# A linear-attention stage: projections in plain fp32 on quarters of the array

## The chip, the cores and the metric

The kernel runs on one core of one Trainium2 chip. The metric is the device time of one execution in microseconds, median over runs; smaller is better. The engines are named as in the profile: PE is TensorE (PEld its weight loads), DVE VectorE, ACT ScalarE, POOL GpSimd, SP the queue that issues most DMAs.

## The reference, cut to what matters

Three layers follow each other: an attention with random features, a soft mixture of experts, and a second mixture. The change touches the first only.

```python
# q, k, v: (4, 8, 576, 64); w_phi: (64, 128)
def phi(x):
    proj = np.einsum('bhsd,df->bhsf', x, w_phi)
    proj = proj - np.max(np.abs(proj), axis=-1, keepdims=True)
    return np.concatenate([np.exp(proj), np.exp(-proj)], axis=-1)
q_p, k_p = phi(q), phi(k)
kv = np.einsum('bhsf,bhsd->bhfd', k_p, v)
z = np.sum(k_p, axis=2)
num = np.einsum('bhsf,bhfd->bhsd', q_p, kv)
den = np.einsum('bhsf,bhf->bhs', q_p, z)[..., None] + 1e-06
return num / den
```

The result, 2304 tokens of 512, goes into `_moe_ref` (logits against `phi`, softmax over tokens and over slots, eight experts on 4 slots each) and then `_moe2_ref` (eight experts of 512 x 1024 on all tokens).

## The kernel before, in words

The 2304 tokens are 18 blocks of 128. A batch has 576 tokens, so blocks 4 and 13 straddle two batches. The attention stage is one loop (lines 444 to 505) in which iteration `i` works on block `i` of k and on block `t = i - 7` of q: iterations 0 to 6 have k alone, up to 17 both, from 18 on q alone.

A block of k or q comes transposed as 128 x 512 fp32 (`kt`, `qt`): 128 rows are the 64 features of two heads, and four pairs `p` of heads stand side by side. `wbd` is a block-diagonal 128 x 256 matrix with `w_phi` twice, so that one product projects both heads of a pair. `split` (lines 120 to 131) makes a high part in fp32r (ACT) and a low part (POOL, for the first two k blocks DVE); `project` (133 to 152) adds three products for each pair: high by high, high by the low part of `wbd`, low by high. A PSUM tile holds four heads, `hh` the first or second half of the eight. DVE takes the largest absolute value of each head off (lines 148 and 150), ACT makes the exponentials.

For k, `kv_acc` adds up v times the features in PSUM over the blocks of a batch, two heads side by side in the column halves of the array, and `z_acc` adds the features up in SBUF (on POOL; while `t < LAG` POOL and DVE take half each). At a batch's end `kv_finish` turns the sums: `kvp` multiplies them by `bd`, which holds an identity and the routing matrix `phi` of the next layer, `zc` brings the z sums into columns; both go into `kvs`, 97 columns for each head.

For q, `q_transpose` turns the projected block by products with an identity, and `q_num` multiplies its exponentials by `kvs` (line 271), for each batch in the block apart; then DVE divides, sums the logits and writes the attention's output `x`. `slot_inputs` turns groups of four blocks into the slots' inputs between these steps.

In this part a planner at compile time decides the order on each engine, from its own costs and the order of the program; after the loop (line 506) the order of the program holds. Loads are issued by SP in order: k, v, q, and 1 MB units of the mixtures' weights among them, into buffers that come free as the stage goes on (`wk` after the last k block, `wq` after the last q block). The next stage begins at line 510.

Of the kernel before, what the change touches and what calls it, by code (L numbers as in the profile page):

```python
# [7 lines left out]
F32 = mybir.dt.float32  # L8
F32R = mybir.dt.float32r
# [6 lines left out]
F = 128  # L16
# [37 lines left out]
def tile_kernel(ctx: ExitStack, tc: tile.TileContext, a):  # L54
# [46 lines left out]
    kt_t, qt_t, vt_t = {}, {}, {}  # L101

    def load_k(t):
        x = kp.tile([128, 512], F32, tag="kt", name=f"kt{t}")
        SP.dma_start(out=x, in_=a["kT"][t])
        kt_t[t] = x

# [3 lines left out]
        vt_t[i] = x  # L111

    def load_q(t):
        x = qp.tile([128, 512], F32, tag="qt", name=f"qt{t}", bufs=2)
        SP.dma_start(out=x, in_=a["qT"][t])
        qt_t[t] = x

    parts = {}

    def split(src, pool, nm, t):  # L120

        hi = pool.tile([128, 512], F32R, tag=f"{nm}h", name=f"{nm}h{t}", bufs=1)
        lo = pool.tile([128, 512], F32R, tag=f"{nm}l", name=f"{nm}l{t}", bufs=1)
        if nm == "k" and t == 0:
            V.tensor_copy(out=hi, in_=src)
        else:
            A.copy(out=hi, in_=src)
        yield
        (V if nm == "k" and t < 2 else G).tensor_tensor(out=lo, in0=src, in1=hi.bitcast(F32), op=ALU.subtract)
        parts[nm, t] = hi, lo  # L130
        yield

    def project(pool, nm, t):

        hi, lo = parts.pop((nm, t))
        pss, us = [], []
        for hh in range(2):
            ps = mm(f"p{nm}{t}_{hh}")
            for j in range(2):
                p = 2 * hh + j  # L140
                o, s = ps[:, j * 256:(j + 1) * 256], slice(p * 128, (p + 1) * 128)
# [3 lines left out]
            pss.append(ps)  # L145
        for hh in range(2):
            m = pool.tile([128, 4], F32, tag=f"m{nm}", name=f"m{nm}{t}_{hh}", bufs=4)
            V.tensor_reduce(out=m, in_=h4(pss[hh]), axis=AX.X, op=ALU.max, apply_absolute_value=True)
            u = pool.tile([128, 512], F32, tag=f"u{nm}", name=f"u{nm}{t}_{hh}", bufs=2)
            V.tensor_tensor(out=h4(u), in0=h4(pss[hh]), in1=m.unsqueeze(2).to_broadcast([128, 4, F]), op=ALU.subtract)  # L150
# [5 lines left out]
    kvacc = {}  # L156

    def k_project(t):
        uk_t[t] = project(kp, "k", t)

    def k_exp(t):
        us = uk_t.pop(t)
        phik = kp.tile([128, H, 2, F], F32, tag="phik", name=f"phik{t}")
        for hh in range(2):
# [36 lines left out]
    def kv_finish(b):  # L201

        acc = kvacc.pop(b)
        kvt = kp.tile([128, 1024], F32, tag="kvt", name=f"kvt{b}", bufs=1)
        for i in range(2):
            A.copy(out=kvt[:, i * 512:(i + 1) * 512], in_=acc[:, i * 512:(i + 1) * 512])
        yield
        zs = zs_t.pop(b)
        zp = mm(f"zp{b}")
        for g in range(4):  # L210
            PE.matmul(zp[32 * g:32 * g + 32, :], ones[:, 0:32], zs[:, g * 512:(g + 1) * 512], start=True, stop=True)
        zrow = kp.tile([128, 512], F32, tag="zrow", name=f"zrow{b}", bufs=1)
        V.tensor_copy(out=zrow, in_=zp)
        kvs = qp.tile([128, 2, H, XW], F32, tag=f"kvs{b % 2}", name=f"kvs{b}", bufs=1)
        for p in range(4):
            ps = mm(f"kvp{b}_{p}")
            for c in range(2):
                PE.matmul(ps[:, c * 192:(c + 1) * 192], kvt[:, p * 256 + c * 128:p * 256 + (c + 1) * 128], bd[:, p], start=True, stop=True)  # L218
            src = ps[:, 0:384].rearrange("p (c h w) -> p c h w", c=2, h=2)
            for c in range(2):  # L220
                dst = kvs[:, c, 2 * p:2 * p + 2, 0:XW - 1]
                if c == 0:
                    A.copy(out=dst, in_=src[:, c])
                else:
                    V.tensor_copy(out=dst, in_=src[:, c])
        zc = mm(f"zc{b}")
        for j in range(2):
            for c in range(2):
                o = (j * 2 + c) * 4
                PE.matmul(zc[:, o:o + 4], zrow[:, j * 256 + c * 128:j * 256 + (c + 1) * 128], sel_e, start=True, stop=True)  # L230

        for c in range(2):
            V.tensor_copy(
                out=kvs[:, c, :, XW - 1].rearrange("p (g j) -> p j g", j=2),
                in_=zc[:, 0:16].rearrange("p (j c g) -> p j c g", j=2, c=2)[:, :, c, :],
            )
        kvs_t[b] = kvs
        yield

    def q_project(t):  # L240
        uq_t[t] = project(qp, "q", t)

    def q_transpose(t, hh):
        ps = mm(f"ut{t}_{hh}")
# [15 lines left out]
    def q_num(t, hh):  # L260
        if hh == 0:
            x_t[t] = const.tile([128, DM], F32, tag=f"x{t % XR}", name=f"x{t}", bufs=1)
        phiq = phiq_t.pop((t, hh))
        if hh == 0:
            lgh_t[t] = qp.tile([128, H, NS], F32, tag="lgh", name=f"lgh{t}", bufs=1)
        lgh = lgh_t[t]
        ps = mm(f"num{t}_{hh}")
        for b, r0, r1 in parts_of(t):
            for j in range(4):
                for c in range(2):  # L270
                    PE.matmul(  # L271
                        ps[r0:r1, j * XW:(j + 1) * XW],
                        phiq[:, c, j * 128 + r0:j * 128 + r1],
                        kvs_t[b][:, c, 4 * hh + j, :],
                        start=c == 0, stop=c == 1,
                    )
# [12 lines left out]
        def x_part():  # L289
            (in_order(V) if held else V).tensor_tensor(  # L290
                out=x_t[t][:, hh * 256:(hh + 1) * 256].rearrange("p (h d) -> p h d", h=4),
                in0=pv[:, :, 0:D], in1=rd.to_broadcast([128, 4, D]), op=ALU.mult,
            )

        if held:
            held_x.append(x_part)
        else:
            x_part()
# [95 lines left out]
        V.tensor_tensor(out=cc, in0=cc, in1=rm.to_broadcast([128, n, NS]), op=ALU.mult)  # L394

    load_k(0)
    wbd = kp.tile([128, 512], F32, tag="zrow", name="wbd", bufs=1)[:, 0:2 * F]
    SP.dma_start(out=wbd, in_=a["wbd"])
    load_k(1)
    load_v(0)  # L400
# [14 lines left out]
    wbdh = qp.tile([128, 2 * F], F32R, name="wbdh", bufs=1)  # L415
    wbdl = qp.tile([128, 2 * F], F32R, name="wbdl", bufs=1)
    A.copy(out=wbdh, in_=wbd)
    V.tensor_tensor(out=wbdl, in0=wbd, in1=wbdh.bitcast(F32), op=ALU.subtract)
# [12 lines left out]
    def k_split(t):
        return split(kt_t.pop(t), kp, "k", t) if t < NT else iter(())

    def q_split(t):
        return split(qt_t.pop(t), qp, "q", t) if 0 <= t < NT else iter(())

    LAG = 7
    for _ in k_split(0):
        pass
    k_project(0)  # L440
    for _ in k_split(1):
        pass
    k_exp(0)
    for i in range(NT + LAG + 1):
        t = i - LAG
# [14 lines left out]
        if i + 1 < NT:  # L460
# [585 lines left out]
```

## Time and profile before

| | us |
|---|---|
| median of 3 runs | 1073.94 |
| lowest, highest | 1071.92, 1074.38 |
| span of the profiled execution | 1066.3 |
| PE busy in it | 1039.9 |
| DVE busy | 734.3 |
| POOL busy | 688.3 |
| ACT busy | 571.5 |

The span runs from the first to the last instruction that was recorded; the runs' times hold what lies around it as well. The profiled execution has no other time than its span; the median stands 7.6 us above it. Matmuls are pipelined and their ends are modelled, so PE's busy time is not work alone; distances from one start to the next are of more use.

### The profile page before, as it was taken

Reading aid. Unit: us, or ns where it says so; the run is one execution under the profiler, and the core shown is the slowest. Engines: PE = TensorE matmul, PEld = TensorE weight load, DVE = VectorE, ACT = ScalarE, POOL = GpSimd, SP = SyncE. Lnnn points to the kernel's source line nnn. Section 1 sums busy time; section 2 is a strip of 40 time slices with the busy share of each in tenths; the row PEclk is TensorE's granted clock in tenths of the full one; section 3 lists DMA queues with packets and bytes.
Section 4 is the critical chain, followed back from the end, with each engine's and each line's share of the span. In section 5 each row is a group of like instructions: output and inputs, shape, how many; then the busy total and the mean of one; then the engine's idle time right before and its main releaser. Section 6 shows DMA issues by size and latency. Waiting matters only on the chain.

```text
span 1066.3 us, 23151 instructions
## 1 busy us (share of the span) xinstructions
PE 1039.9 (98%) x9206; PEld 974.1 (91%) x9206; DVE 734.3 (69%) x1518; ACT 571.5 (54%) x1009; POOL 688.3 (65%) x442
## 2 busy tenths in 40 slices
PE   7999999999899999999999999999999999999998
PEld 5688878963799999999999999999999999999998
DVE  6878787850578867667666767676667667676765
ACT  5665544412556666665556555554655565555542
POOL 4776561106656776777778578767867785787543
PEclk9999999999999999999999999999999999999999
DMA  8773215469400040022003100400210031000111
GB/s 261 252 278 88 60 35 184 166 263 409 190 2 1 2 159 1 2 82 78 2 1 120 41 2 2 159 2 1 90 70 1 2 120 41 2 1 21 56 45 61
DMA packets 22571, 89.26 MB, mean 84 GB/s; under 512 B 2752, under 2 KB 5568, under 8 KB 14272
## 3 DMA queue, kind: packets, MB, share of 16 engines
q1 hardware_dynamic: 22176, 87.26, 22.8%
q8 instruction: 73, 1.20, 0.5%
q0 software_dynamic: 288, 0.52, 0.2%
q14 instruction: 34, 0.28, 0.1%
HBM read 83.05 MB, written 4.72 MB: 82 GB/s over the span
## 4 chain that ended last, share of the span: by engine, by line
PE 90%; DVE 4%; POOL 2%; issue 2%; DMA 2%; ACT 1%; SPq 0%; DVEq 0%; POOLq 0%; ACTq 0%
PE x L50 36%; PE y L50 18%; PE z L50 15%; PE num L271 6%; PE kvacc L179 2%; PE ut L246 1%; PE ps L50 1%; PE kvp L218 1%; DMA moe_w<-in_moe_w 1%; PE ph L50 1%; PE pk L142 1%; PE pk L144 1%; POOL zs L197 1%; PE pq L142 1%; PE pq L144 1%
## 5 line engine op out<-in xcount | busy, mean ns | idle before, releaser
L50 POOL TENSOR_TENSOR hl_s<-s,hh_s 128x512 fp32r<-128x512 f32 x288 | 367.5, 1298 | 215.9 <-ACT hh_s L50 195.8
L50 ACT ACTIVATE hh_s<-s 128x512 fp32r<-128x512 f32 x288 | 176.3, 630 | 55.5 <-DVE s L50 51.6
L50 PE MATMUL x<-w_t,hh_s 128*128 128x256 f32 x1152 | 204.2, 277 | 0.0
L50 ACT ACTIVATE r<-z 128x512 f32<-128x512 f32 x144 | 86.2, 599 | 165.6 <-PE z L50 165.3
L50 PEld LDWEIGHTS x<-w_t,hh_s 128*128 128x128 f32 x1152 | 173.5, 188 | 0.1
L50 DVE SCALAR_TENSOR_TENSOR xo<-x,P,xo 128x256 f32<-128x256 f32 x252 | 120.8, 479 | 70.6 <-PE x L50 70.6
L50 ACT ACTIVATE hh_a<-z 128x512 fp32r<-128x512 f32 x216 | 122.3, 600 | 74.9 <-DVE s L50 74.1
L50 PE MATMUL x<-w_t,hl_s 128*128 128x256 f32 x576 | 159.2, 276 | 0.0
L50 DVE SCALAR_TENSOR_TENSOR s<-z,r 128x512 f32<-128x512 f32 x144 | 98.8, 686 | 86.5 <-ACT hh_a L50 81.7
L50 DVE SCALAR_TENSOR_TENSOR hl_a<-z,hh_a 128x512 fp32r<-128x512 f32 x216 | 147.1, 681 | 0.0
L50 PEld LDWEIGHTS x<-w_t,hl_s 128*128 128x128 f32 x576 | 108.2, 188 | 0.0
L50 PE MATMUL x<-w_t,hh_a 128*128 128x256 f32 x576 | 101.9, 277 | 2.8 <-DVE xo L50 2.8
L50 PE MATMUL z<-w_b,hh_a 128*128 128x256 f32 x576 | 102.8, 278 | 0.0
L50 PE MATMUL y<-w_t,hh_s 128*128 128x256 f32 x576 | 102.6, 277 | 0.0
L50 DVE SCALAR_TENSOR_TENSOR s<-z,s 128x512 f32<-128x512 f32 x144 | 98.5, 684 | 5.6 <-POOL hl_s L50 3.4
L50 PE MATMUL x<-w_b,hh_a 128*128 128x256 f32 x576 | 101.7, 276 | 0.1
L50 PE MATMUL y<-w_b,hh_s 128*128 128x256 f32 x576 | 101.5, 276 | 0.0
L50 PEld LDWEIGHTS x<-w_t,hh_a 128*128 128x128 f32 x576 | 86.7, 188 | 3.2 <-DVE xo L50 3.2
L50 PEld LDWEIGHTS z<-w_b,hh_a 128*128 128x128 f32 x576 | 86.8, 188 | 2.9 <-issue 2.9
L50 PEld LDWEIGHTS y<-w_t,hh_s 128*128 128x128 f32 x576 | 87.4, 188 | 0.0
L50 PEld LDWEIGHTS x<-w_b,hh_a 128*128 128x128 f32 x576 | 86.8, 188 | 0.4 <-ACT hh_a L50 0.4
L50 PEld LDWEIGHTS y<-w_b,hh_s 128*128 128x128 f32 x576 | 86.7, 188 | 0.0
(213 smaller groups left out, 2335.8 us busy)
## 6 DMA issues: line engine op xcount, KB each, us to landing
moe_w<-in_moe_w SPq DMA_DIRECT2D x64, 1024.0 KB, 6.9
vt<-in_vb SPq DMA_DIRECT2D x20, 256.0 KB, 3.8
kt<-in_kT SPq DMA_DIRECT2D x18, 256.0 KB, 3.6
qt<-in_qT SPq DMA_DIRECT2D x18, 256.0 KB, 2.8
out<-xo SPq DMA_DIRECT2D x18, 128.0 KB, 1.7
out<-xo SPq DMA_DIRECT2D x9, 256.0 KB, 2.0
rep<-in_rep POOLq DMA_DIRECT2D x2, 256.0 KB, 5.8
bd<-in_bd SPq DMA_DIRECT2D x1, 384.0 KB, 3.9
```

The costliest lines, as they stand in the source:

```text
L50: return lambda *args, **kwargs: self.tc.keep_in_program_order(make(*args, **kwargs))
L142: PE.matmul(o, hi[:, s], wbdh, start=True, stop=False)
L144: PE.matmul(o, lo[:, s], wbdh, start=False, stop=True)
L179: PE.matmul(acc[64 * j:64 * j + 64, p * 256:(p + 1) * 256], v[:, (2 * p + j) * D:(2 * p + j + 1) * D], phik[:, 2 * p + j].rearrange("p c f ...
L197: G.tensor_tensor(out=z[r0:r1, 0:cut], in0=z[r0:r1, 0:cut], in1=flat[r0:r1, 0:cut], op=ALU.add)
L218: PE.matmul(ps[:, c * 192:(c + 1) * 192], kvt[:, p * 256 + c * 128:p * 256 + (c + 1) * 128], bd[:, p], start=True, stop=True)
L246: PE.transpose(ps[:, j * 128:(j + 1) * 128], uq_t[t][hh][:, j * 128:(j + 1) * 128], ident)
L271: PE.matmul(ps[r0:r1, j * XW:(j + 1) * XW], phiq[:, c, j * 128 + r0:j * 128 + r1], kvs_t[b][:, c, 4 * hh + j, :], start=c == 0, stop=c == 1,)
```

## The change

The splits and the tiles for them go, and so do the products of high and low parts. `project` multiplies plain fp32 blocks: for each pair `p`, each of its two heads `j` (the upper or lower 64 rows of the array) and each half `g` of the 128 tokens (64 columns of the array) there is one product of 64 x 64 by 128 columns. Head `j` of each pair goes to PSUM tile `j`, so a tile now holds the even or the odd heads, and everything behind it (`k_exp`, `kvs`, the numerators, the output) deals heads out in that way. `kvp` is cut into quarters likewise, with PSUM tiles for each `c` and `j` instead of each pair; `zc` and the numerators are cut into two halves of 64 columns, which alternate, in all blocks, not only in straddling ones. `kt` and `qt` have 4 buffers instead of 2; `wbd` has a tile of its own.

```diff
-    def split(src, pool, nm, t):
...
-    def project(pool, nm, t):
...
-                PE.matmul(o, hi[:, s], wbdh, start=True, stop=False)
-                PE.matmul(o, hi[:, s], wbdl, start=False, stop=False)
-                PE.matmul(o, lo[:, s], wbdh, start=False, stop=True)
...
+    def project(pool, nm, x, t):
+
+        pss, us = [mm(f"p{nm}{t}_{j}") for j in range(2)], []
+        for p in range(4):
             for j in range(2):
...
+                r = slice(j * D, (j + 1) * D)
+                for g in range(2):
+                    PE.matmul(
+                        pss[j][g * 64:(g + 1) * 64, p * F:(p + 1) * F],
+                        x[r, p * 128 + g * 64:p * 128 + (g + 1) * 64], wbd[r, j * F:(j + 1) * F],
+                        start=True, stop=True,
+                    )
...
-                A.activation(out=phik[:, 4 * hh:4 * hh + 4, c, :], in_=h4(us[hh]), func=AF.Exp, scale=1.0 if c == 0 else -1.0)
+        for j in range(2):
             for c in range(2):
+                A.activation(out=phik[:, j::2, c, :], in_=h4(us[j]), func=AF.Exp, scale=1.0 if c == 0 else -1.0)
...
+        for c in range(2):
+            pss = [mm(f"kvp{b}_{c}_{j}") for j in range(2)]
+            for p in range(4):
+                for j in range(2):
+                    r = slice(j * D, (j + 1) * D)
+                    for g in range(2):
+                        f = p * 256 + c * 128 + g * 64
+                        PE.matmul(
+                            pss[j][g * 64:(g + 1) * 64, p * 96:(p + 1) * 96],
+                            kvt[r, f:f + 64], bd[r, p, j * 96:(j + 1) * 96], start=True, stop=True,
+                        )
+            for j in range(2):
+                (A.copy if j == 0 else V.tensor_copy)(
+                    out=kvs[:, c, j::2, 0:XW - 1], in_=pss[j][:, 0:384].rearrange("p (h w) -> p h w", h=4),
+                )
...
+                for g in range(2):
+                    f = j * 256 + c * 128 + g * 64
+                    PE.matmul(zc[g * 64:(g + 1) * 64, o:o + 4], zrow[:, f:f + 64], sel_e, start=True, stop=True)
...
+        for j in range(4):
+            for c in range(2):
+                for g in range(2):
+                    b = (128 * t + 64 * g) // S
                     PE.matmul(
...
+                        ps[g * 64:(g + 1) * 64, j * XW:(j + 1) * XW],
+                        phiq[:, c, j * 128 + g * 64:j * 128 + (g + 1) * 64],
+                        kvs_t[b][:, c, 2 * j + hh, :],
                         start=c == 0, stop=c == 1,
                     )
```

## Rows read from the trace of the kernel before

**Rows 1.** The page: busy time by engine; the chain by engine.
```profile
PE 1039.9 (98%) x9206; PEld 974.1 (91%) x9206; DVE 734.3 (69%) x1518; ACT 571.5 (54%) x1009; POOL 688.3 (65%) x442
...
PE 90%; DVE 4%; POOL 2%; issue 2%; DMA 2%; ACT 1%; SPq 0%; DVEq 0%; POOLq 0%; ACTq 0%
```

**Rows 2.** Table by stretch; the first line names the columns.
```profile
core 0: us, PE busy (x) PEld busy (x) DVE busy (x) ACT busy (x) POOL busy (x), PEclk, DMA share, GB/s
18.40:38.90 20.50, 17.35 (x118) 11.69 (x116) 17.91 (x20) 14.50 (x27) 17.89 (x9) 1.00 0.86 291
...
69.66:97.64 27.98, 27.98 (x243) 25.14 (x242) 20.92 (x49) 15.69 (x30) 18.69 (x8) 1.00 0.56 192
...
222.00:270.00 48.00, 43.83 (x481) 20.35 (x479) 13.38 (x61) 11.61 (x24) 22.19 (x18) 1.00 0.95 384
```

**Rows 3.** Order of time, PE, 78.9 to 88.4: start, duration of the group, records.
```profile
78.99 0.37 PE L142 MATMUL pk<-wbdh,kh 128*128 128x256 f32 x1
79.20 0.28 PE L143 MATMUL pk<-wbdl,kh 128*128 128x256 f32 x1
79.32 0.28 PE L144 MATMUL pk<-wbdh,kl 128*128 128x256 f32 x1
...
80.52 0.60 PE L246 MATMUL ut<-ident,uq 128*128 128x128 f32 x4
80.95 1.92 PE L271 MATMUL num<-kvs,phiq 128*128 128x97 f32 x16
82.71 0.60 PE L246 MATMUL ut<-ident,uq 128*128 128x128 f32 x4
83.07 0.36 PE L142 MATMUL pq<-wbdh,qh 128*128 128x256 f32 x1
...
84.45 0.28 PE L144 MATMUL pq<-wbdh,ql 128*128 128x256 f32 x1
84.66 1.95 PE L179 MATMUL kvacc<-phik,vt 128*64 128x256 f32 x16
86.53 2.03 PE L271 MATMUL num<-kvs,phiq 128*128 128x97 f32 x16
88.34 0.36 PE L142 MATMUL pk<-wbdh,kh 128*128 128x256 f32 x1
```

**Rows 4.** Order of time, DVE, the same iteration.
```profile
79.25 0.16 DVE L280 TENSOR_SCALAR rd<-num 128x4 f32<-128x4 f32 x1 [1.95 <-PE num L271]
...
88.60 0.16 DVE L280 TENSOR_SCALAR rd<-num 128x4 f32<-128x4 f32 x1 [1.95 <-PE num L271]
```

**Rows 5.** Order of time, PE and DVE, one q-only iteration.
```profile
176.32 1.92 PE L271 MATMUL num<-kvs,phiq 128*128 128x97 f32 x16
...
182.09 0.58 PE L271 MATMUL num<-kvs,phiq 128*128 128x97 f32 x4
...
180.48 0.16 DVE L280 TENSOR_SCALAR rd<-num 128x4 f32<-128x4 f32 x1 [0.62 <-PE num L271]
```

**Rows 6.** Order of time, POOL and DVE, 18 to 26.
```profile
18.32 1.27 POOL L129 TENSOR_TENSOR kl<-kt,kh 128x512 fp32r<-128x512 f32 x1
19.55 3.35 POOL L197 TENSOR_TENSOR zs<-zs,phik 128x1024 f32<-128x1024 f32 x1
22.86 1.28 POOL L129 TENSOR_TENSOR kl<-kt,kh 128x512 fp32r<-128x512 f32 x1
...
18.43 2.24 DVE L199 TENSOR_TENSOR zs<-zs,phik 128x1024 f32<-128x1024 f32 x1
20.59 1.28 DVE L148 TENSOR_REDUCE mk<-pk 128x4 f32<-128x512 f32 x2
```

**Rows 7.** Order of time, PE, a batch's end.
```profile
120.75 1.07 PE L211 MATMUL zp<-zs,ones 128*32 128x512 f32 x8
121.75 2.87 PE L218 MATMUL kvp<-bd,kvt 128*128 128x192 f32 x16
124.45 0.73 PE L230 MATMUL zc<-sel_e,zrow 128*128 128x4 f32 x6
```

**Rows 8.** Order of time, PE, numerators of a straddling block.
```profile
99.66 2.60 PE L271 MATMUL num<-kvs,phiq 128*64 128x97 f32 x32
102.20 0.33 PE L246 MATMUL ut<-ident,uq 128*128 128x128 f32 x1
```

**Rows 9.** Groups by line, 0 to 222: busy us, mean ns of one, idle before.
```profile
L129 POOL TENSOR_TENSOR ql<-qt,qh 128x512 fp32r<-128x512 f32 x18 | 23.0, 1279 | 44.1 <-ACT qh L127 44.1
L127 ACT CAST qh<-qt 128x512 fp32r<-128x512 f32 x18 | 11.2, 621 | 1.8 <-issue 1.1 <-PE pq L143 0.7
L193 ACT COPY zs<-phik 128x2048 f32<-128x2048 f32 (+1 forms) x4 | 7.6, 1896 | 4.3 <-PE zp L211 4.3
```

**Rows 10.** Order of time, all engines, the start.
```profile
4.21 0.79 PE L142 MATMUL pk<-wbdh,kh 128*128 128x256 f32 x2 [4.21 <-ACT wbdh L417]
...
6.47 0.69 DVE L148 TENSOR_REDUCE mk<-pk 128x4 f32<-128x512 f32 x1 [1.53 <-PE pk L144]
...
15.98 2.37 POOL L197 TENSOR_TENSOR zs<-zs,phik 128x1024 f32<-128x1024 f32 x1 [1.57 <-ACT phik L166]
```

More of the change, by code (lines that the diff above doesn't have):

```diff
@@ L103, in load_k @@
     def load_k(t):
-        x = kp.tile([128, 512], F32, tag="kt", name=f"kt{t}")
+        x = kp.tile([128, 512], F32, tag="kt", name=f"kt{t}", bufs=4)
         SP.dma_start(out=x, in_=a["kT"][t])
@@ L113, in load_q @@
     def load_q(t):
-        x = qp.tile([128, 512], F32, tag="qt", name=f"qt{t}", bufs=2)
+        x = qp.tile([128, 512], F32, tag="qt", name=f"qt{t}", bufs=4)
         SP.dma_start(out=x, in_=a["qT"][t])
         qt_t[t] = x
-    parts = {}
-    def split(src, pool, nm, t):
[L122 to L131, printed above, removed]
@@ L133, in project @@
-    def project(pool, nm, t):
[L135 to L138, printed above, removed]
-            for j in range(2):
-                p = 2 * hh + j
-                o, s = ps[:, j * 256:(j + 1) * 256], slice(p * 128, (p + 1) * 128)
-                PE.matmul(o, hi[:, s], wbdh, start=True, stop=False)
-                PE.matmul(o, hi[:, s], wbdl, start=False, stop=False)
-                PE.matmul(o, lo[:, s], wbdh, start=False, stop=True)
[L145 to L150, printed above, removed]
+    def project(pool, nm, x, t):
+        pss, us = [mm(f"p{nm}{t}_{j}") for j in range(2)], []
+        for p in range(4):
+            for j in range(2):
+                r = slice(j * D, (j + 1) * D)
[6 more added lines that the diff above has]
+        for j in range(2):
+            m = pool.tile([128, 4], F32, tag=f"m{nm}", name=f"m{nm}{t}_{j}", bufs=4)
+            V.tensor_reduce(out=m, in_=h4(pss[j]), axis=AX.X, op=ALU.max, apply_absolute_value=True)
+            u = pool.tile([128, 512], F32, tag=f"u{nm}", name=f"u{nm}{t}_{j}", bufs=2)
+            V.tensor_tensor(out=h4(u), in0=h4(pss[j]), in1=m.unsqueeze(2).to_broadcast([128, 4, F]), op=ALU.subtract)
@@ L158, in k_project @@
     def k_project(t):
-        uk_t[t] = project(kp, "k", t)
+        uk_t[t] = project(kp, "k", kt_t.pop(t), t)
     def k_exp(t):
@@ L163, in k_exp @@
         phik = kp.tile([128, H, 2, F], F32, tag="phik", name=f"phik{t}")
-        for hh in range(2):
+        for j in range(2):
             for c in range(2):
-                A.activation(out=phik[:, 4 * hh:4 * hh + 4, c, :], in_=h4(us[hh]), func=AF.Exp, scale=1.0 if c == 0 else -1.0)
+                A.activation(out=phik[:, j::2, c, :], in_=h4(us[j]), func=AF.Exp, scale=1.0 if c == 0 else -1.0)
         phik_t[t] = phik
@@ L214, in kv_finish @@
         kvs = qp.tile([128, 2, H, XW], F32, tag=f"kvs{b % 2}", name=f"kvs{b}", bufs=1)
[L215 to L225, printed above, removed]
+        for c in range(2):
[9 more added lines that the diff above has]
+                        )
+            for j in range(2):
+                (A.copy if j == 0 else V.tensor_copy)(
+                    out=kvs[:, c, j::2, 0:XW - 1], in_=pss[j][:, 0:384].rearrange("p (h w) -> p h w", h=4),
+                )
         zc = mm(f"zc{b}")
@@ L240, in q_project @@
     def q_project(t):
-        uq_t[t] = project(qp, "q", t)
+        uq_t[t] = project(qp, "q", qt_t.pop(t), t)
     def q_transpose(t, hh):
@@ L290, in x_part @@
             (in_order(V) if held else V).tensor_tensor(
-                out=x_t[t][:, hh * 256:(hh + 1) * 256].rearrange("p (h d) -> p h d", h=4),
+                out=x_t[t].rearrange("p (h d) -> p h d", h=H)[:, hh::2, :],
                 in0=pv[:, :, 0:D], in1=rd.to_broadcast([128, 4, D]), op=ALU.mult,
@@ L396, in tile_kernel @@
     load_k(0)
-    wbd = kp.tile([128, 512], F32, tag="zrow", name="wbd", bufs=1)[:, 0:2 * F]
+    wbd = qp.tile([128, 2 * F], F32, name="wbd", bufs=1)
     SP.dma_start(out=wbd, in_=a["wbd"])
@@ L414, in tile_kernel @@
     V.tensor_copy(out=sels, in_=sel4[:, 0:NS])
[L415 to L418, printed above, removed]
     def load_units(pool, first, n):
@@ L429, in si_step @@
             si_steps.pop(0)
[L431 to L435, printed above, removed]
     LAG = 7
-    for _ in k_split(0):
-        pass
     k_project(0)
-    for _ in k_split(1):
-        pass
     k_exp(0)
@@ L450, in tile_kernel @@
             load_q(t + 3)
-        ks, qs = k_split(i + 2), q_split(t + 2)
         if i + 1 < NT:
             k_project(i + 1)
-        next(ks, None)
         if 0 <= t < NT:
             q_transpose(t, 0)
-        next(ks, None)
         if 0 <= t - 1 < NT:
@@ L466, in tile_kernel @@
         si_step()
-        next(qs, None)
-        next(qs, None)
         fin = iter(())
```

7 lines of the change are left out of this document (removed).

## The prediction

> **What bounds the kernel now.** I read the page first, then a table by stretch, then TensorE's order of time, then VectorE's and GpSimd's in the same microseconds. The page [rows 1] shows a chain of waits that is 90% TensorE, but this is an average over three stages. The change touches only the attention stage, 0 to 222 us. The table by stretch [rows 2] cuts it up. From 38.9 to 222 TensorE is busy for all but a few us, and one iteration of its order of time [rows 3] shows it packed: from a k projection at 78.99 to the next at 88.34 it goes through k projection, transposes, numerators, transposes, q projection, kv sums, numerators, 9.35 us without a hole. VectorE has holes in the same iteration [rows 4]: 1.95 us ahead of `rd`, waiting for the numerators, so some 7.4 of 9.35 us are used. The q-only iterations [rows 5] take 5.77 us (176.32 to 182.09); there VectorE waits only 0.62 us for numerators, so with its small gaps it is used for 5.0 to 5.1. From 18 to 30 us it is another picture [rows 6]: GpSimd runs split, z sum, split, z sum with no gap (1.27 + 3.3 us, a period of 4.54), and VectorE is full too. After 222 the DMA engines are 95% busy with 384 GB/s (last row of [rows 2]); that stage begins when attention gives up its buffers, so it moves forward as a whole and keeps its length. What the change is worth is therefore what the attention stage loses.
>
> **Parts, on TensorE.** A plain fp32 product stands in the trace as two records, and each takes the time of twice its columns: `kvp`'s, of 192, stand 0.169 apart [rows 7], fp32r ones of 256 only 0.117 [rows 3].
>
> Projections. Before: 12 products of 256 fp32r columns, 0.117 us apart [rows 3], 1.41 us. After: 16 products of 128 columns, 4 in each quarter of the array, 8 records each. A record streams 256 column steps, as an fp32r one does now: 0.107 to 0.117 us, I take 0.109. If the four quarters run beside each other, that is 0.87 us, 0.54 less. That parts of the array run beside each other is shown for columns: four z products on 32 columns each, 512 columns of fp32 (8 records that last some 0.6 us), take 1.00 us to the next product [rows 7], and the kv pairs on 64 columns take 1.87 us for 8 products [rows 3]. For the two halves of the rows no row of before shows it. Bounds: 0.87 us if rows overlap, 1.74 if the row halves take turns, and 2.6 if in addition each weight load of 64 columns (0.055, half of the 0.11 at which the 128-column loads of the numerators pace them [rows 3]) stands exposed: 16 x 0.162. I take 0.87, because the two row halves read different partitions and write different PSUM tiles. In the PE-bound part there are 11 k and 18 q projections: 29 x -0.54 = -15.7 us.
>
> Numerators. Now 16 records of 128 x 128 in 1.76 us [rows 3], 0.11 each, although 97 columns would take 0.085 by `kvp`'s 0.169: the load of 128 weight columns paces them. In the two blocks that straddle a batch the halves already exist, on 64 columns: 32 records in 2.54 us, 0.079 each, so a load of half the columns is hidden; but there one half's records all come ahead of the other's [rows 8]. After, the two halves alternate, as the kv pairs do: 16 records each at 0.082 (between 0.079 and 0.085), 1.31 us, 1.35 with the start. 32 x (1.76 - 1.35) = -13.1, and 4 x (2.54 - 1.35) = -4.8.
>
> A rule to weigh here: the Trainium skill, "TensorE: Matmul & The Clock Gate", section "Part 3: Packing small matmuls — row/col tiling", says that a weight load overlaps a running product only if it goes to another group of rows. By it the numerators would cost 16 x (0.082 + 0.055) = 2.2 us, 0.4 more than now, 32 x 0.4 = 13 us lost in place of 13 won. The 0.079 of [rows 8], all in one set of rows, is against it.
>
> kv and z products [rows 7]. `kvp`: 16 records of 192 columns in 2.70 us; after, 16 records of 96 columns in each quarter, 0.082 each, 1.31: -1.39. `zc`: 8 loads of 128 columns, 0.11 each, in 0.88 us; after, 8 of 64 in each column half, 0.45: -0.43. Three of the four batches lie in the PE-bound part: -5.5.
>
> Switches. Going from the q projection's 128 x 128 to the kv sums' 128 x 64, the next product comes 0.21 us after the last in place of 0.12, and the first two products after such a step stand 0.20 apart in place of 0.12 [rows 3]; 0.12 to 0.17 in all, I take 0.15. Bounds: 0.09, the first of the two alone, and 0.28, a whole product's duration. A full iteration has 2 such steps now and 6 after (quarters, whole, halves, whole, quarters, halves); a q-only one 0 and 5; a batch end one more. 11 x 4 + 8 x 5 + 4 = 88, +13.2 us (+8 to +25).
>
> The Trainium skill, "TensorEngine Tiling (Array Packing)", section "Tiling Modes", says that a change of mode, not of tile, drains the engine. The 0.09 above agrees in kind; by a full drain the term is its upper end, +25, and the sum some 12 us worse.
>
> Sum on TensorE from 38.9 on: -15.7 - 13.1 - 4.8 - 5.5 + 13.2 = -25.9.
>
> **Parts, elsewhere.** The splits go: 35 casts of 0.62 us on ScalarE and 34 subtractions of 1.28 on GpSimd [rows 9]. After 39 us both engines have idle time, so this is worth nothing there. From 18 to 30 it takes 1.27 of GpSimd's 4.54 us, and the z sum is late next: its VectorE half takes 2.24 us beside GpSimd's work where 1024 fp32 elements take about 1.2 (twice the 0.6 step of the 512-element instructions); VectorE's own loop is 4 x 0.6 + 1.2 to 2.2 = 3.6 to 4.6, I take 4.2, 0.3 less for some four iterations, -1.2. At the start the second tile's split holds things up: VectorE reduces the first tile at 6.47, GpSimd's first z sum starts at 15.98 [rows 10]. Without splits TensorE starts at about 3.8 instead of 4.21 and nothing waits for a cast: VectorE has two tiles done at about 5.5 + 2 x 2.4 = 10.3, and ScalarE the eight exponentials (0.55 apart) and the 1.9 us copy [rows 9] between them at about 13.5, against 15.98. I take -2.5 (bounds 0 and -5). The loads issue earlier, since k and q get 4 buffers instead of 2; every 256 KB load still stands behind the same weights on SP's queue, and DMA is 86% busy there [rows 2], which caps this gain. The first batch's kv end falls here too, half covered: -0.8. Together -4.5.
>
> **Given back.** The z sums and kv sums now wait for all four exponentials of a block (heads are dealt out alternately), two of 0.62 us more than before; GpSimd, without the splits, is then busy 4.5 of 8 us and has room for that. VectorE's bound: 7.4 us against TensorE's new 9.35 - 1.08 - 0.82 + 0.6 = 8.05; q-only 5.0 against 5.77 - 0.54 - 0.82 + 0.75 = 5.16. So VectorE would be 92 to 97% used, and in the q-only stretch it, not TensorE, is next late. Nothing ran at 97% before except VectorE at 18 us; I give back 0.25 an iteration, +5.
>
> Total: -25.9 - 4.5 + 5 = -25.4. The profiled span is 1066.3; the runs' median is 7.6 us above it, for what lies around the span, and I keep that: 1073.94 - 25.4 = 1048.5, say 1048.
>
> **Rivals.** (1) VectorE and GpSimd become the bound. For it: [rows 6] and the 5.0 of 5.16. Against: 1.95 us of holes in each of 11 long iterations. If the long ones reach only 8.7 (half of the gain) and the q-only ones 5.5, with nothing from the start: 11 x 0.65 + 8 x 0.27 + 5 for batches and straddling = 14, so 1060. The order that the planner writes out anew could do the same. (2) The row halves take turns: the one that ends slower. Place: the 29 projections and 4 `kvp`. For it: no row of before has a 64-row product; against: column parts overlap freely. At 1.74 us per projection the sum is 29 x 0.33 - 17.9 - 1.3 + 13.2 - 2 = +1.6, no change; with loads exposed, 2.6 us, it is 29 x 1.19 - 17.9 - 2.8 + 13.2 - 2 = +25, 1099. It decides from about 1.7 us per projection upward; midway 1087. (3) Switches at 0.09, the start at -5 and nothing given back: 1048 - 5.3 - 2.5 - 5 = 1035; [rows 3] has the smaller price, but also the late second product. (4) The quarters bring what they should, but the time is spent waiting elsewhere in attention, no change: the holes on VectorE speak against it.
>
> **Numbers.** Forecast, 1040 to 1056: 0.55. Rival 1, 1056 to 1070: 0.22. Rival 2, 1075 to 1099: 0.12, of it 0.02 within the bound. Rival 3, 1030 to 1040: 0.08. Rival 4: 0.03. A measurement here tells about 0.2% (2.1 us) from no change. Faster 0.85, same 0.05, slower 0.10. The range 1036 to 1070 leaves out half of rival 3 and rivals 2 and 4.
>
> **What would show it.** A q projection of 0.9 us from its first product to the next group's, numerators of 1.35, `kvp` of 1.3, a full iteration near 8.1 and a q-only one near 5.2 us, the stretch of full DMA that opens the middle stage beginning near 197 instead of 222 [rows 2], and a middle stage as long as before. Wrong if a projection takes 1.7 or more, if a switch costs over 0.2, if a full iteration stays at 8.7 us with VectorE's holes gone, or if the stages after attention change in length.

## The result, and the profile after

The changed kernel takes 1045.99 us (median of 4 runs, 1045.20 to 1048.79) against 1072.93 (1070.33 to 1074.38): a ratio of 0.9758 with a 95% interval of [0.9738, 0.9778], 26.9 us less. The kernel before has a fourth run here, of 1070.33, so its median is no longer the 1073.94 of the first three. The profiled execution's span went from 1066.3 to 1043.4. The page of after answers to [rows 1]:

```profile
PE 1011.8 (97%) x10662; PEld 934.1 (90%) x10662; DVE 728.1 (70%) x1506; ACT 550.8 (53%) x965; POOL 643.4 (62%) x408
...
PE 87%; DVE 7%; issue 2%; DMA 2%; POOL 1%; ACT 1%; SPq 0%; DVEq 0%; ACTq 0%; POOLq 0%
```

VectorE's share of the chain rises from 4% to 7%: the first sign that it is now late somewhere. The stretches of [rows 2] follow, with the same columns. The first is of the same microseconds as there, the second holds the same three iterations, and the third begins 25.3 us earlier:

```profile
18.40:38.90 20.50, 18.29 (x258) 10.55 (x258) 17.55 (x24) 10.57 (x18) 11.29 (x5) 1.00 0.88 315
...
59.68:83.50 23.82, 23.82 (x461) 19.33 (x457) 20.46 (x49) 13.56 (x27) 11.17 (x3) 1.00 0.45 147
...
196.70:245.00 48.30, 44.14 (x483) 20.68 (x481) 13.37 (x61) 11.79 (x25) 22.19 (x18) 1.00 0.95 381
```

The same k projections took 27.98 us before (69.66 to 97.64) and take 23.82 now. GpSimd, without the splits, is busy 11.29 of 20.50 us at the start, not 17.89. The DMA-bound stretch shows the same load as before. Its first weight load is issued at 198.30, not 222.15, which is 23.9 us earlier; the first product of the middle stage (`ph`) goes from 229.78 to 204.48, 25.3 earlier.

One long iteration on TensorE, against [rows 3] (start, duration of the group, records):

```profile
67.62 1.10 PE L125 MATMUL pk<-wbd,kt 64*64 64x128 f32 x32
68.65 0.66 PE L236 MATMUL ut<-ident,uq 128*128 128x128 f32 x4
69.24 1.55 PE L262 MATMUL num<-kvs,phiq 128*64 128x97 f32 x32
70.72 0.66 PE L236 MATMUL ut<-ident,uq 128*128 128x128 f32 x4
71.31 1.10 PE L125 MATMUL pq<-wbd,qt 64*64 64x128 f32 x32
72.35 1.95 PE L163 MATMUL kvacc<-phik,vt 128*64 128x256 f32 x16
74.12 1.50 PE L262 MATMUL num<-kvs,phiq 128*64 128x97 f32 x32
75.56 0.34 PE L125 MATMUL pk<-wbd,kt 64*64 64x128 f32 x4
```

67.62 to 75.56 is 7.94 us; it was 9.35. VectorE's hole ahead of `rd` shrinks from the 1.95 of [rows 4], but not to nothing:

```profile
67.74 0.16 DVE L271 TENSOR_SCALAR rd<-num 128x4 f32<-128x4 f32 x1 [0.74 <-PE num L262]
...
75.68 0.16 DVE L271 TENSOR_SCALAR rd<-num 128x4 f32<-128x4 f32 x1 [0.67 <-PE num L262]
```

The batch end, against [rows 7]:

```profile
106.85 1.55 PE L206 MATMUL kvp<-bd,kvt 64*64 64x96 f32 x64
108.33 0.64 PE L220 MATMUL zc<-sel_e,zrow 128*64 128x4 f32 x16
108.81 1.06 PE L163 MATMUL kvacc<-phik,vt 128*64 128x256 f32 x8
```

`kvp` now takes 1.48 us to the next group, `zc` 0.48. A q-only iteration, TensorE and then VectorE, against [rows 5]:

```profile
154.85 1.56 PE L262 MATMUL num<-kvs,phiq 128*64 128x97 f32 x32
156.99 0.63 PE L236 MATMUL ut<-ident,uq 128*128 128x128 f32 x4 [0.58 <-DVE uq L134]
157.55 1.56 PE L262 MATMUL num<-kvs,phiq 128*64 128x97 f32 x32
159.03 0.66 PE L236 MATMUL ut<-ident,uq 128*128 128x128 f32 x4
159.62 1.10 PE L125 MATMUL pq<-wbd,qt 64*64 64x128 f32 x32
160.65 0.30 PE L262 MATMUL num<-kvs,phiq 128*64 128x97 f32 x2
```

```profile
154.96 1.29 DVE L132 TENSOR_REDUCE mq<-pq 128x4 f32<-128x512 f32 x2 [0.57 <-PE pq L125]
156.16 1.28 DVE L134 TENSOR_TENSOR uq<-pq,mq 128x512 f32<-128x512 f32 x2
```

154.85 to 160.65 is 5.80 us, no better than the 5.77 before, though TensorE's groups are shorter. The two engines wait for each other in turn: VectorE 0.57 us for the projection, then TensorE 0.58 for the subtraction `uq`. Both PSUM tiles of a projection are now complete only at its end (head `j` of every pair goes to tile `j`), and VectorE then does both reductions (x2) before the first subtraction.

A loss that has grown stands where `slot_inputs` meets a k block of the next batch. There VectorE forms `mx`, the running maximum, and `dg`, a diagonal matrix of it, and TensorE waits for `dg` to make the product `gmb` (all engines, in order of time):

```profile
90.26 1.50 PE L262 MATMUL num<-kvs,phiq 128*64 128x97 f32 x32
...
90.30 4.50 POOL L181 TENSOR_TENSOR zs<-zs,phik 64x2048 f32<-64x2048 f32 x1 [4.30 <-ACT phik L150]
...
92.03 2.80 DVE L318 TENSOR_SCALAR dg<-ident,mx 32x32 f32<-32x32 f32 x1
...
94.98 0.37 PE L327 MATMUL gmb<-dg,ones 32*128 32x32 f32 x2 [3.21 <-DVE rd L271]
```

`dg` has 32 x 32 elements and lasts 2.80 us; it ends 0.03 us after GpSimd's z sum (94.83 and 94.80). TensorE stands for 3.21 us, and then runs slower. At the second such place the z sum lasts from 133.36 to 137.87, and the small instruction that ends with it is `mx`:

```profile
135.09 2.80 DVE L316 TENSOR_TENSOR mx<-mx,mx 128x1 f32<-128x1 f32 x1
...
138.30 0.37 PE L327 MATMUL gmb<-dg,ones 32*128 32x32 f32 x2 [3.48 <-DVE rd L271]
```

The table by stretch has the granted clock in its third column from the right. It is 1.00 at 2.4 GHz and 0.50 at 1.2 GHz; behind both places, and in two stretches of the middle stage, it is 0.50:

```profile
95.40:98.80 3.40, 3.40 (x44) 2.74 (x46) 3.40 (x10) 1.06 (x3) 0.00 (x0) 0.50 0.02 5
139.80:143.20 3.40, 3.40 (x40) 2.84 (x39) 2.08 (x10) 1.36 (x5) 0.00 (x0) 0.50 0.02 5
...
245.60:249.00 3.40, 3.40 (x33) 1.36 (x32) 0.34 (x2) 1.31 (x2) 3.40 (x2) 0.50 0.24 34
252.40:259.20 6.80, 6.26 (x28) 5.60 (x28) 3.33 (x7) 3.58 (x7) 1.97 (x2) 0.50 0.99 408
```

The granted clock is 0.50 in 17.0 us of this execution; 0.5 x 17.0 / 1043.4 = 0.008, and its mean is indeed 0.992. The profiled execution of before has no such stretch before its last 2 us and a mean of 0.999.

### The profile page after: what moved, and what is told of

It reads as the page before. It is cut to its first block, busy times and chain, and to the rows that moved or that the text cites. A ratio compares the mean times of both kernels' runs of the same rounds, so it can differ in the third digit from the quotient of the medians.

```text
span 1043.4 us, 25949 instructions
## 1 busy us (share of the span) xinstructions
PE 1011.8 (97%) x10662; PEld 934.1 (90%) x10662; DVE 728.1 (70%) x1506; ACT 550.8 (53%) x965; POOL 643.4 (62%) x408
## 3 DMA queue, kind: packets, MB, share of 16 engines
q1 hardware_dynamic: 22176, 87.26, 22.9%
## 4 chain that ended last, share of the span: by engine, by line
PE 87%; DVE 7%; issue 2%; DMA 2%; POOL 1%; ACT 1%; SPq 0%; DVEq 0%; ACTq 0%; POOLq 0%
PE x L50 37%; PE y L50 18%; PE z L50 16%; PE num L262 4%; PE kvacc L163 2%; PE ut L236 2%; DMA moe_w<-in_moe_w 2%; PE pq L125 1%; PE ps L50 1%; PE pk L125 1%; DVE mq L132 1%; PE ph L50 1%; DVE uq L134 1%; DVE uk L134 1%; PE po L50 1%
## 5 line engine op out<-in xcount | busy, mean ns | idle before, releaser
L181 POOL TENSOR_TENSOR zs<-zs,phik 128x2048 f32<-128x2048 f32 (+3 forms) x16 | 60.6, 3785 | 58.1 <-ACT phik L150 55.3
```

The lines of the kernel that those rows point to most:

```text
L181: G.tensor_tensor(out=z[r0:r1, 0:cut], in0=z[r0:r1, 0:cut], in1=flat[r0:r1, 0:cut], op=ALU.add)
```

## Experiments

| kernel | median us (range) | ratio to before | mean clock of its runs | `ph` at |
|---|---|---|---|---|
| after | 1045.99 (1045.20–1048.79) | 0.9758 [0.9738, 0.9778] | 0.987–0.992 | 204.5 |
| as_changed | 1047.28 (1045.13–1048.43) | 0.9773 [0.9759, 0.9788] | 0.987–0.992 | 206.8 |
| rows_in_turn | 1050.34 (1047.51–1052.18) | 0.9789 [0.9752, 0.9825] | 0.992–1.000 | 214.3 |
| whole_projections | 1062.35 (1060.76–1064.20) | 0.9910 [0.9880, 0.9940] | 0.995–0.996 | 221.3 |
| whole_numerators | 1053.97 (1053.07–1055.62) | 0.9833 [0.9805, 0.9861] | 0.994–0.996 | 214.2 |
| two_buffers | 1048.89 (1048.56–1049.38) | 0.9784 [0.9758, 0.9811] | 0.985–0.989 | 208.2 |
| z_pieces | 1044.03 (1040.46–1045.08) | 0.9733 [0.9713, 0.9754] | 0.990–0.998 | 202.1 |
| first_half_first | 1042.53 (1040.48–1044.69) | 0.9725 [0.9706, 0.9745] | 0.990–0.996 | 202.8 |
| kept_busy | 1044.29 (1041.50–1045.97) | 0.9742 [0.9721, 0.9763] | 0.993–0.998 | 205.8 |
| all_three | 1041.32 (1040.11–1042.39) | 0.9714 [0.9696, 0.9731] | 0.992–0.996 | 200.5 |
| two_fixes | 1039.91 (1039.66–1041.07) | 0.9710 [0.9697, 0.9724] | 0.993–0.996 | 200.6 |
| three_again | 1039.84 (1039.20–1041.12) | 0.9709 [0.9696, 0.9722] | 0.993–0.998 | 200.4 |
| before_pieces | 1064.83 (1063.93–1066.32) | 0.9940 [0.9927, 0.9952] | 0.995–1.000 | 225.2 |

The clock column is the lowest and highest mean granted clock of a kernel's runs, and `ph` is of its one profiled execution. Most of the spread within one kernel goes with its clock. From a kernel's run of highest clock to that of lowest: before 1068.05 (1.000) to 1076.40 (0.989), after as as_changed 1045.13 (0.992) to 1048.43 (0.987), z_pieces 1040.46 (0.998) to 1045.08 (0.990), kept_busy 1041.50 (0.998) to 1045.97 (0.993). That is 0.6 to 0.9 us for each 0.001; a line through all runs of the kernels in the table, each kernel's own mean taken off, has 0.6 (correlation -0.84). Medians are compared below with that in mind. `ph` varies as well: after and as_changed are the same kernel, and their `ph` are 2.3 us apart. Steadier is the distance from the first q projection to `ph`, where no extra stretch of slow clock falls into it: 165.3 us in after and in kept_busy, against 166.9 in as_changed, which has a stretch at 0.50 more, at 171.5.

### Do the two row halves run beside each other?

**rows_in_turn** finishes one half of the rows before the other:

```diff
-        for p in range(4):
-            for j in range(2):
+        for j in range(2):
+            for p in range(4):
```

> The loop over the two heads of a pair stands outside the loop over the pairs, so all products on the upper 64 rows come ahead of those on the lower 64. If the gain of a projection rests on the row halves running beside each other, it now takes 2 x 0.87 = 1.74 us instead of 0.87: long iterations 7.94 + 1.74 = 9.7 us (11 of them, +19), q-only ones up to 0.87 longer (+6), time near 1071 us. If the array picks products for the lower rows out of the queue all the same, or if TensorE is no longer what is waited for, long iterations stay under 8.5 us and the time is 1046 to 1053.

```profile
75.49 1.59 PE L125 MATMUL pq<-wbd,qt 64*64 64x128 f32 x32
77.01 0.44 PE L163 MATMUL kvacc<-phik,vt 128*64 128x256 f32 x2
```

A projection takes 1.52 us to the next group, not 1.03, and a long iteration 8.91 us, between the 8.5 and the 9.7 of the two expectations; `ph` comes 9.8 us later and the median is 4.4 longer, part of it hidden by a higher clock (0.996 on average against 0.990). In the changed kernel the four records of a group start 7 ns apart and groups 0.109 us apart: the quarters do run beside each other. Even in turn it is 1.52 and not 1.74 with the switch on top: by the spacing of the records, the second half begins at 75.99, 0.50 us after the first, while three of the first half's eight steps of 0.109 us are still to come.

**whole_projections** drops the quarters and keeps plain fp32:

```diff
-                r = slice(j * D, (j + 1) * D)
-                for g in range(2):
-                    PE.matmul(
...
+                PE.matmul(pss[j][:, p * F:(p + 1) * F], x[:, p * 128:(p + 1) * 128], wbd[:, j * F:(j + 1) * F], start=True, stop=True)
```

> Plain fp32 without splits, but projections on the whole array: 8 products of 128 x 128 by 128 columns for a block, the zeros of the block-diagonal matrix included. If the quarters make the gain in the long iterations, a projection takes 16 x 0.11 = 1.76 us, paced by the weight load, long iterations 9.4 us, time near 1067; what the missing splits brought at the start stays (first q projection near 39 us). If the gain is that casts and subtractions are gone from ScalarE and GpSimd, the time stays within 5 us of 1046.

```profile
69.64 1.95 PE L123 MATMUL pq<-wbd,qt 128*128 128x128 f32 x16
71.52 0.44 PE L157 MATMUL kvacc<-phik,vt 128*64 128x256 f32 x2
```

1.88 us per projection, 0.85 more than in quarters, and a long iteration of 9.49 us: longer than before the change. Its 1062.35 is under the 1067 expected, since part of the loss is hidden: a q-only iteration lengthens by 0.53 us and not by 0.85 (6.27 against 5.74), and the two iterations at the first wait for `gmb` do not lengthen at all (11.43 and 15.37 us against 11.79 and 15.39), as that wait is now 1.46 us and the clock does not fall behind it. For the projection itself plain fp32 alone is a loss (1.88 us against the 1.59 from one group to the next in [rows 3]); the quarters make it pay.

### The numerators, and the buffers

**whole_numerators** goes back to whole blocks (`for b, r0, r1 in parts_of(t)` as the outer loop in place of `for g in range(2)` as the inner).

> Numerators on all 128 columns again (by batch in straddling blocks), everything else as changed. TensorE's account: 1.76 instead of 1.31 us for each, one switch less in a long iteration: +0.75 x 11, +3 for the straddling blocks, and in q-only iterations 0.9 more work against four switches less and 0.7 us of waiting, +0 to 0.3: 1057 to 1060. If VectorE has become the bound, the time stays at 1046 to 1049.

```profile
75.82 2.03 PE L261 MATMUL num<-kvs,phiq 128*128 128x97 f32 x16
77.77 1.10 PE L125 MATMUL pk<-wbd,kt 64*64 64x128 f32 x32
```

1.95 us against 1.44 to the next group of the same kind, 8.68 against 7.94 per long iteration, as expected, and 8.0 us in the median: under the 11 to 14 expected, since again the two iterations at the first wait for `gmb` do not lengthen (11.62 and 14.57 us; the wait is 0.95).

**two_buffers** sets `bufs=2` for `kt` and `qt` again.

> kt and qt with 2 buffers as in the kernel before, everything else as changed. If the 6.6 us that the first q projection comes earlier (39.2 instead of 45.8) are the missing splits', it stays at 39 to 41 us and the time at 1046 to 1048. If they are the earlier loads', the first q projection goes back to 44 us or later and the time to 1051 to 1053.

It takes 2.9 us more in the median than after, 1.6 more than as_changed. Its first q projection starts at 40.47 instead of 39.20, but the four profiles with four buffers and the same instructions up to there (after, as_changed, kept_busy, first_half_first) have it anywhere from 39.10 to 40.59. So no gain of the early loads shows. Some 1.8 us go with its clock (0.987 on average; 0.003 x 0.6).

### Where the change is held back

**z_pieces** cuts GpSimd's z sum, so that VectorE need not wait for all of it:

```diff
-            G.tensor_tensor(out=z[r0:r1, 0:cut], in0=z[r0:r1, 0:cut], in1=flat[r0:r1, 0:cut], op=ALU.add)
+            for s in range(0, cut, 512):
+                G.tensor_tensor(out=z[r0:r1, s:s + 512], in0=z[r0:r1, s:s + 512], in1=flat[r0:r1, s:s + 512], op=ALU.add)
```

> GpSimd's z sum in pieces of 512 columns instead of one of 1024 or 2048; the rest as changed. In the changed kernel VectorE's dg (92.03, 2.80 us) and mx (135.09, 2.80 us) end with GpSimd's z sum, TensorE then stands for 3.5 and 3.7 us and its granted clock is 0.5 for 3.4 us behind each. If VectorE waits for the GpSimd instruction that is under way, these waits are at most a piece, 1.3 us, TensorE's gaps under 2.3 us, the clock stays at 1.0 there, and the time falls by 4 to 7 us, to 1039 to 1042. If GpSimd's pieces follow each other without letting VectorE in, or the waits have another cause, the two waits and the time stay (1045 to 1047).

```profile
92.10 5.00 POOL L182 TENSOR_TENSOR zs<-zs,phik 64x512 f32<-64x512 f32 x4 [4.30 <-ACT phik L150]
...
93.84 0.80 DVE L319 TENSOR_SCALAR dg<-ident,mx 32x32 f32<-32x32 f32 x1
...
94.78 0.38 PE L328 MATMUL gmb<-dg,ones 32*128 32x32 f32 x2 [1.50 <-DVE rd L272]
```

`dg` falls from 2.80 to 0.80 us and ends 0.04 after the second of the four pieces; TensorE's wait falls from 3.21 to 1.50. Behind it the clock stays at 1.00:

```profile
96.00:100.00 4.00, 4.00 (x92) 3.26 (x88) 4.00 (x13) 2.30 (x5) 1.10 (x1) 1.00 0.00 0
```

In all five profiles with the whole z sum and otherwise the changed order (after, as_changed, kept_busy, first_half_first, two_buffers) the clock falls to 0.50 between 95 and 97; in none of the four with pieces. So at this place the clock's fall goes with the uncut sum. The length of the wait alone does not decide it: in rows_in_turn, whose sum is whole too, TensorE waits 1.58 us, hardly longer than here, and the clock falls for 6.8 us:

```profile
99.96 0.37 PE L327 MATMUL gmb<-dg,ones 32*128 32x32 f32 x2 [1.58 <-DVE rd L271]
...
100.70:107.50 6.80, 6.80 (x69) 5.67 (x64) 4.63 (x15) 3.77 (x8) 0.00 (x0) 0.50 0.02 4
```

At the second place the pieces help less. `mx`, `dg` and one more small instruction of VectorE now wait for a piece each (0.79, 1.20 and 1.28 us), TensorE's wait only goes from 3.48 to 2.73, and the clock still falls behind it, at 136.2:

```profile
135.90 0.37 PE L328 MATMUL gmb<-dg,ones 32*128 32x32 f32 x2 [2.73 <-DVE dg L319]
```

The time falls by 2.0 us, less than the 4 to 7 expected, and two medians 1.96 apart with overlapping intervals would not settle even that; nor would `ph`, 2.4 earlier. The iterations do: from one k projection to the next, the one with the first stall lasts 11.8 us in after, as_changed, kept_busy and first_half_first, and 10.2 in all four profiles with pieces; the one behind it 15.4 and 13.8.

**before_pieces** makes the same edit in the kernel before.

> The kernel before with GpSimd's z sum in pieces of 512 columns. There the same waits of VectorE (3.28 us at 106.49, 3.03 at 153.97) leave TensorE gaps of 1.5 and 2.75 us, and the granted clock does not fall. If the gaps cost what they last, 2 to 3 us are won, about 1070; if the pieces only slow GpSimd, which is full from 18 to 30 us and makes the splits there, 1072 to 1075.

It was expected to gain 2 to 3 us and gained 6.8 (about 1 of it a higher clock; `ph` comes 4.6 earlier): the miss is in size. `dg` was already held up there, 3.28 us, ending 0.04 after GpSimd, and TensorE's waits ahead of `gmb` were 1.27 us here and 2.37 at the second place:

```profile
105.22 4.51 POOL L197 TENSOR_TENSOR zs<-zs,phik 64x2048 f32<-64x2048 f32 x1 [3.87 <-ACT phik L166]
...
106.49 3.28 DVE L327 TENSOR_SCALAR dg<-ident,mx 32x32 f32<-32x32 f32 x1
...
109.92 0.37 PE L336 MATMUL gmb<-dg,ones 32*128 32x32 f32 x2 [1.27 <-DVE rd L280]
...
158.38 0.38 PE L336 MATMUL gmb<-dg,ones 32*128 32x32 f32 x2 [2.37 <-DVE rd L280]
```

So this wait is older than the change; `dg` took 1.26 us with pieces. With the pieces in both kernels the change is worth 20.8 us (1064.8 to 1044.0), not 26.9. At an equal clock it would be some 2.5 us more, since z_pieces ran at 0.993 on average and before_pieces at 0.997.

**first_half_first** keeps VectorE's order of the program in the q-only projections, so that the first half is subtracted before the second is reduced:

```diff
+            D_ = in_order(V) if nm == "q" and t > NT - LAG else V
...
-            V.tensor_reduce(out=m, in_=h4(pss[j]), axis=AX.X, op=ALU.max, apply_absolute_value=True)
+            D_.tensor_reduce(out=m, in_=h4(pss[j]), axis=AX.X, op=ALU.max, apply_absolute_value=True)
```

(and the subtraction likewise).

> For the last q blocks the order on VectorE is held as maximum and subtraction of the even heads, then of the odd ones (the planner writes maximum, maximum, subtraction, subtraction). If the q-only iterations (5.74 us, with 0.74 us of TensorE waiting for the first turned half) are a loop of waits through projection, VectorE and transposes, the half arrives 0.6 us earlier and six iterations fall to about 5.2 us: 1042 to 1043. If VectorE's sum of work is the bound there, they stay at 5.6 to 5.8: 1045 to 1047.

```profile
154.75 1.56 PE L263 MATMUL num<-kvs,phiq 128*64 128x97 f32 x32
156.42 0.63 PE L237 MATMUL ut<-ident,uq 128*128 128x128 f32 x4
...
160.08 1.56 PE L263 MATMUL num<-kvs,phiq 128*64 128x97 f32 x32
```

TensorE's wait at `ut` is gone, and a q-only iteration takes 5.33 us, close to the 5.16 of the prediction. The loop of two waits was the cause, not VectorE's total work. From the first q projection to `ph` it brings 1.6 us (165.3 to 163.7); the median falls by 3.5, as expected, but part of that is a higher clock.

**kept_busy** adds 8 transposes of the identity ahead of `p_sot` and 8 behind its copies (`keep_busy(True, 8)`), so that TensorE does not stand there, at about 245 us.

> Eight idle transposes ahead of the products that spread the slots' outputs (p_sot) and eight behind them. In the changed kernel the granted clock is 0.5 at 245.6 to 249.0 and 252.4 to 259.2 us, behind holes of TensorE, and 2.3 of the 25.3 us gained are given back there; in the kernel before the same holes did not lower it. If the holes in front of p_sot and behind it are what lowers the clock, it stays at 1.0 and the time falls by 2 to 3 us, to 1043 to 1044. If the earlier holes (1.4 us at 234.6) or the loads decide, or the clock falls later instead, 1045 to 1047.

The middle stage had no slow stretch in its profile and the clock of its runs is higher, but that can be chance: as_changed, the changed kernel unaltered, has one of 6.8 us there, and z_pieces and first_half_first, which fill no gap, have none.

> The changed kernel once more, with nothing altered, on the chip on which the next one runs. If the clock's fall at 245 to 259 us belongs to the changed kernel's order, it stands in this profile again and the middle and last stages take 2.3 us longer than before; if it is chance, it is missing and these stages are as long as before. The falls at 95 and 140 us, behind TensorE's gaps of 3.5 us and more, stand again by either theory. Time 1044 to 1047.

as_changed says how firm the result is: 1047.28, ratio 0.9773, and again no run over 0.992 in clock. **all_three** puts the three edits together.

> The z sum in pieces, the held order on VectorE for the last q blocks and the idle transposes together. If their causes are apart, the gains add: 5.5 + 3.5 + 2.3 = 11 us, about 1035. If each only moves the same wait, no more than the largest alone, 1039 to 1042.

1041.32 with an interval apart from that of after, but not the 1035 of the full sum. Whether the added transposes have a part in it, the last two kernels tell: **two_fixes** is all_three without them, **three_again** all_three once more, on the same chip.

> The z sum in pieces of 512 columns and the first half first, without the sixteen filling products in the middle stage; three_again on the same chip is the same kernel with them. Theory: TensorE's granted clock falls to 1.2 GHz in the middle stage (before 260 us) because TensorE stands idle between the small products there, and the filling products prevent it; then the mean granted clock of the runs is lower here than in three_again by 0.002 to 0.004, and the time about 1.5 to 2.5 us longer: 1043 to 1044, three_again 1041 to 1042. Rival: the stretches at 1.2 GHz come and go from run to run whatever fills those gaps; then both kernels have the same spread of mean clocks and their medians lie within 1 us of each other, 1041 to 1043. Either way the runs of one kernel should be longer by some 0.6 us for each 0.001 that their mean granted clock is lower, as in the kernels so far.

> All three edits once more, beside two_fixes. Theory: 1041 to 1042, with a mean granted clock 0.002 to 0.004 above that of two_fixes. Rival: no difference from two_fixes in clock, and none over 1 us in time.

1039.91 and 1039.84, clocks of 0.993 to 0.996 and 0.993 to 0.998: the rival holds, the added transposes are worth nothing that shows. The other two gains add up: from the first q projection to `ph` z_pieces takes 3.1 us off the 165.3, first_half_first 1.6, and the three kernels with both 4.6 to 4.7 (to 160.6). In two_fixes a slow stretch stands in the middle stage:

```profile
95.00:98.40 3.40, 3.40 (x72) 2.90 (x72) 3.21 (x10) 1.71 (x4) 2.11 (x2) 1.00 0.02 5
...
256.40:259.80 3.40, 3.40 (x18) 3.40 (x18) 2.62 (x6) 1.57 (x4) 1.51 (x2) 0.51 0.00 0
```

The version to keep is two_fixes: 6 us under the changed kernel, 31 under the one before.

## Why the prediction was right

The forecast was 1048, the time is 1046, and the mechanism is the one forecast: TensorE's groups in the attention stage became shorter, and that stage was what the time hung on. Undone one at a time, the quartered projections cost 16.4 us and the halved numerators 8.0, together some 24 of the 26.9. That attention ends 25.3 us earlier, where the sum was 25.4, is luck: in as_changed, the same kernel, it is 22.9 (`ph` at 206.8). By its steps:

**Projections.** Groups stand 0.109 us apart as taken, and 1.03 to the next group is 0.87 and a switch of 0.16. rows_in_turn and whole_projections show that neither bound of the turn-taking rival was near.

**Numerators, `kvp`, `zc`.** 1.48 to the next group is 1.31 and 0.17; 1.48 for `kvp` likewise; `zc` 0.48 against 0.45. The loads of 64 columns are hidden within one set of rows, as [rows 8] had it: pairs of records, one in each half, stand 0.083 us apart. No run undoes `kvp` and `zc`; their shares are read from the rows alone.

**Switches.** 0.13 to 0.23 each, against the 0.15 taken, within its bounds: 0.16 behind a projection, 0.13 and 0.17 behind numerators, and 0.15 to 0.23 on four transposes, which took 0.36 to 0.44 us to the next group and take 0.59. The Trainium skill, "TensorEngine Tiling (Array Packing)", section "Tiling Modes", says that a change of mode drains the engine. The rows agree in kind; the price here is under the 0.28 that the prediction took for a full drain.

**Long iterations.** 7.94 measured against 8.05, and none of the 0.25 given back: VectorE keeps a hole of 0.7 us.

**q-only iterations: mis-sized.** 5.16 plus 0.25 was forecast, 5.74 to 5.80 measured for an iteration without `slot_inputs`, no gain at all; the two longer ones between them did gain (8.25 and 7.79 us before, 7.39 and 6.24 now). The step said that VectorE would be next late, for its total of 5.0 us. In fact both halves of a projection finishing together made a loop of two waits; with the order mended the same work runs in 5.3.

**Start: mis-sized the other way.** -4.5 forecast, -6.6 measured (the first q projection from 45.83 to 39.20; -5.2 to -6.7 in the four profiles named at two_buffers). VectorE starts to reduce at 5.98 instead of 6.47, and GpSimd's first z sum at 15.04, not the 13.5 of the step. The parts are only roughly known. whole_projections has the first q projection at 42.44, so 1.9 to 3.3 us of it belong to the quarters. The earlier loads have no share that shows. The remaining 3.4 us fit the missing splits, which no run takes by themselves.

**Given back: too small, and in the wrong place.** The +5 was spread over all iterations. From the first q projection to `ph` the kernel is 18.7 us faster (184.0 to 165.3), where the sum has 25.9 less 5, 20.9; if the parts hold, 7.2 were given back. It lies in the q-only iterations without `slot_inputs` (0.6 each above 5.16), in the two stalls behind GpSimd (TensorE's waits ahead of `gmb` were 1.27 and 2.37 us before, and are 3.21 and 3.48), and in the slow clock behind them. What was missed here and what was missed at the start cancelled.

**From the span to the runs.** The prediction took the 7.6 us between the span and the median for what lies around the span. Each run's time is only 1.7 to 2.1 us over its own span (2.7 in one run). Some 2.4 us more come from the clock: the profiled execution had a mean of 0.999 where before's runs have 0.995 in the middle. The rest is that 1073.94 was a high median of three runs; later sets of before have medians of 1071.1 to 1072.5. By the same estimate of 0.6 us for each 0.001, at a clock of 0.995 before is at 1072.0 and after at 1043.7: the change itself is worth some 28 us, and the lower clock that it is granted costs 3.

**The middle stage** was to keep its length, and a change of it was one of the prediction's signs of being wrong. Its DMA-bound part does keep it; from `ph` to the end the profiled execution takes 2.5 us more (836.47 to 838.96), with the slow clock of the stretches at 245.6 and 252.4. What brings them there stays open. Such stretches stand in after, as_changed, two_buffers, all_three and two_fixes, and some 55 us behind `ph` also in whole_projections, whole_numerators and before_pieces; there are none in the kernel before, rows_in_turn, kept_busy, z_pieces, first_half_first and three_again. So they belong neither to the changed order nor to unfilled gaps alone, and part of the 2.5 us may be chance.

## What to carry to other kernels

When products are split over parts of the array, price the record spacing and the switches from rows of the same kernel, and then look at which consumer now gets all its tiles at once: here the order behind the product cost 1.6 us. When TensorE gets faster, look for long instructions on GpSimd that run beside short ones of VectorE on TensorE's path, and cut them: here that brought 6.8 us in the kernel before and stayed cheap, 5.00 us for four pieces against 4.50 in one. Compare medians together with the mean granted clock of the runs; here a difference of 0.005 was worth 3 us.

## What the runs showed of the hardware

**Some of VectorE's instructions wait for GpSimd's to end.** `dg` took 2.80 and 3.28 us beside a z sum of 4.5 us in one piece, and 0.80 beside pieces of 1.25. Not all wait: beside the same z sum of after, the subtractions `uq` at 90.52, which read PSUM, took their usual 0.64 us each. The halves of z on VectorE show it too: one takes 1.21 us alone and 2.18 where GpSimd's own half ran until 20.71, 1.09 before VectorE's end:

```profile
19.62 2.18 DVE L183 TENSOR_TENSOR zs<-zs,phik 128x1024 f32<-128x1024 f32 x1
...
24.11 1.21 DVE L183 TENSOR_TENSOR zs<-zs,phik 128x1024 f32<-128x1024 f32 x1
```

The prediction read the same 2.24 us of [rows 6] as slow progress beside GpSimd, and so missed what it would do to `dg`. The Trainium skill, "SBUF — State Buffer", section "SBUF: two separate sides", states that GpSimd and those instructions of VectorE that have two inputs in SBUF or run in a two-port mode share one pair of ports, as an exclusive lock for a whole instruction. The trace agrees: the halves of z and `mx` have two inputs in SBUF, and they end as above. `dg` reads one matrix and one column there; no run shows under which of the two conditions it waits.

**Half a clock behind a stall, but not behind each.** In after, TensorE ran at 1.2 GHz for 3.4 us behind its waits of 3.21 and 3.48 us. It also ran at 1.2 GHz behind 2.73 us in z_pieces, 1.58 and 1.84 us in rows_in_turn, and 1.58 us in as_changed (at 170.5). It stayed at 2.4 GHz behind 1.57 us at that same place in after, behind 1.50 us in z_pieces, and behind 1.27 and 2.37 us in the kernel before. So the length of a wait does not decide it; what does stays open here.
